# Top-k attention with a mixture of depths: the last keys turned into another bank, the scores in halves of 288 keys behind the values

## The chip, the cores and the metric

The kernel runs on one core of a Trainium2 chip. The core's engines work side by side, each through its own list of instructions in order, and wait for one another by semaphores: TensorE (matrix products and turns, results into PSUM), ScalarE (ACT), VectorE (DVE), GpSimd (POOL) and SyncE (SP, which issues transfers). The metric is device time in microseconds (us).

## The reference

Attention for 8 batches, 8 heads, 576 tokens of 64 numbers, all in float32. In each row of scores only the 32 largest count. Then a layer that works on the 128 tokens of a batch with the highest gate.

```
scores = q @ k.T / sqrt(64)
kth    = 32nd largest of each row
attn   = softmax(where(scores >= kth, scores, -1e9))
x      = concat over heads of attn @ v          # (8, 576, 512)
gate   = x @ w_gate
idx    = the 128 tokens of a batch with the largest gate
out    = x;  out[idx] = x[idx] + sigmoid(gate[idx]) * relu(x[idx] @ w1) @ w2
```

## The kernel before, in words

The work is cut into units `(b, t, hp)`: batch, query block and pair of heads, 8 x 5 x 4 = 160. For t = 0 to 3 a unit has two tiles, 128 queries of each head of the pair, by 576 keys. For t = 4 it has one, the last 64 queries of both heads together. J is 4, P is 128, R is 64, JP is 512, S is 576. Keys are taken as 512 ("0:JP") and the last 64 ("JP:S").

The main loop (line 590) is a pipeline written out by hand. In step `n` the engines do, for different units:

- TensorE, in this order: `turn` of z of unit n-3, tile 0 (four 128x128 transposes into `ptr`); `values` of unit n-4, tile 0 (products of pT and v into `av`); `turn` of tile 1; `turn_last`, which turns the last 64 keys of both tiles in one transpose; the scores of unit n+1 against 512 keys (`multiply`); `values` of tile 1; the scores against the last 64 keys. Then what a load step or a mixture step has.
- ScalarE: `part` (sides, the sign of score less bound) for n-1, the exponentials of n-3 (`pT` twice, then `last`), a first half of z for n-2, `keep` (scores of n+1 out of PSUM, `sc<-ps`), `keep_values` (`xs<-av`), then the copies of loads and mixture.
- GpSimd: `mask` for n-1 (y, with eight more numbers, "steps"), the second half of z for n-2, every fourth step `normalise` (x), then `cut` (`seen<-best`) for n and `lift` (`seen<-next`) for n-1.
- DVE: `find_bound` for n (32 largest by parts), `find_kth` for n-1, and parts of the mixture.

The next step's `sides` need this step's `cut`; z on ScalarE needs `lift`; z on GpSimd needs z on ScalarE; `turn` needs z on GpSimd.

PSUM has eight banks of 512 float32 a partition. The scores' tile `ps` has four (lines 84, 606), `ptr` two, `av` one, and one is shared in turn by the loads' turns and all steps of the mixture (`ps_misc`, tag "misc"). In `ps` the first tile's scores lie at 0 to 576, the second's at 1472 to 2048 (last 64 keys first), and `turn_last` writes at 896 to 1024, so into the bank that also has the first tile's last 64 keys:

```
tr = ps[0 : n * R, 1024 - P : 1024]
```

In nine of a batch's 20 steps the next batch's k and q are turned (`load_qkv`: TensorE `tr<-ident`, ScalarE `kqT<-tr`), and the mixture of the batch before goes on by one piece a step (`mixture`: xe_ps, extra_ps, h_ps twice, y_ps). Wrappers keep the program's order on TensorE, ScalarE, DVE and GpSimd (class `InOrder`); all their instructions stand under line 41 in the profile. The function `general` is a second way for inputs on which the fast search for the bound fails; it is not taken here.

Of the kernel before, what the change touches and what calls it, by code (L numbers as in the profile page):

```python
# [11 lines left out]
FP32 = mybir.dt.float32  # L12
# [32 lines left out]
def kernel(  # L45
# [104 lines left out]

    def room_for_qkv(b):

        return kqpool.tile([P, 2, NHP, S], FP32, name="kqT"), vbufs[b % 2]

    def load_qkv(qb, kb, vb, kqT, vs):

        last = [ldpool.tile([R, H, D], FP32, name=f"last{i}", bufs=1) for i in range(2)]
        for rows, src in zip(last, (kb, qb)):
            nc.sync.dma_start(out=rows, in_=src[:, JP:S, :].rearrange("h p d -> p h d"))

        def fetch(i):
            hp, src = i // 2, (kb, qb)[i % 2]
            rows = ldpool.tile([P, J, 2, D], FP32, name="rows")
            for hh in range(2):
                nc.sync.dma_start(
                    out=rows[:, :, hh, :],
                    in_=src[2 * hp + hh, 0:JP, :].rearrange("(p j) d -> p j d", j=J),
                )
            return rows

        fetched = [fetch(i) for i in range(3)]
        vt, vlast, vpair = vs
        v_rows = vb[:, JP:S, :].rearrange("h p d -> p h d")
        nc.sync.dma_start(out=vlast[:, :, 0:D], in_=v_rows)
        for hh in range(2):
            nc.sync.dma_start(
                out=vpair[hh * R : (hh + 1) * R, :, hh, 0:D], in_=v_rows[:, hh::2, :]
            )
        tr = ps_misc.tile([P, 512], FP32, name="tr", tag="misc")
        for i in range(2 * NHP):  # L180
            w, hp = divmod(i, NHP)
            pe.transpose(
                tr[:, i * R : (i + 1) * R],
                last[w][:, 2 * hp : 2 * hp + 2, :].rearrange("p h d -> p (h d)"),
                ident[0:R, 0:R],
            )
        act.copy(
            out=kqT[:, :, :, JP:S],
            in_=tr.rearrange("p (w c r) -> p w c r", w=2, c=NHP),
        )  # L190
        yield
        for i in range(2 * NHP):
            tr = ps_misc.tile([P, 512], FP32, name="tr", tag="misc")
            for c in range(J):
                pe.transpose(
                    tr[:, c * P : (c + 1) * P],
                    fetched[i][:, c, :, :].rearrange("p h d -> p (h d)"),
                    ident,
                )
            act.copy(out=kqT[:, i % 2, i // 2, 0:JP], in_=tr)  # L200
            if i + 3 < 2 * NHP:
                fetched.append(fetch(i + 3))
            nc.sync.dma_start(
                out=vt[:, i, :, 0:D],
                in_=vb[i, 0:JP, :].rearrange("(p j) d -> p j d", j=J),
            )
            yield

    def heads_of(t):

        return [[(0, 0), (1, R)]] if t == J else [[(0, 0)], [(1, 0)]]

    def multiply(t, hp, kqT, ps, keys):

        n = R if t == J else P
        for at, heads in zip((0, 1536) if keys.start == 0 else (JP, 1536 - R), heads_of(t)):
            for hh, r in heads:
                d = slice(hh * D, (hh + 1) * D)
                pe.matmul(
                    ps[r : r + n, at : at + keys.stop - keys.start],
                    kqT[d, 1, hp, t * P : t * P + n],
                    kqT[d, 0, hp, keys],
                )  # L230

    def keep(n, ps):

        sc = scpool.tile([P, 2, S], FP32, name="sc")
        for i in range(n):
            at = i * (4 * 512 - S)
            act.copy(out=sc[:, i, :], in_=ps[:, at : at + S])
        return sc

    def find_bound(n, sc):  # L240
# [69 lines left out]
            pe.transpose(tr[:, c * P : (c + 1) * P], z[:, i, at : at + P], ident)  # L310
        return tr

    def turn_last(n, z, ps):

        last = z.rearrange("p i s -> p (i s)")[:, JP : JP + n * R]
        tr = ps[0 : n * R, 1024 - P : 1024]
        pe.transpose(tr, last, ident)
        return tr

    def values(t, hp, i, pT, last, av, vs):  # L320

# [125 lines left out]
    def mixture(row0, x, gate, rank, exact=False):  # L447
# [51 lines left out]
        for t in range(NT):  # L499
            n = R if t == J else P  # L500
            pe.matmul(
                ps[:, 0:2],
                pick[0:n, t, :],
                extra[0:n, t, :],
                start=(t == 0),
                stop=(t == J),
            )
        row_i = modpool.tile([P, 1], I32, name="row_i", bufs=2)

        dve.tensor_scalar_min(out=row_i, in0=ps[:, 0:1], scalar1=float(B * S - 1))  # L510
        g = modpool.tile([P, 1], FP32, name="g")
        dve.tensor_copy(out=g, in_=ps[:, 1:2])

        hT = modpool.tile([P, NFC, CAP], FP32, name="hT")
        for f0 in range(0, NFC, 4):
# [19 lines left out]
                ps, hT[:, fc, :], w2[:, fc, :], start=(fc == 0), stop=(fc == NFC - 1)  # L535
            )
        gy = modpool.tile([P, HD], FP32, name="gy")
        act.activation(gy, ps, AF.Copy, scale=g)

        nc.gpsimd.indirect_dma_start(  # L540
            out=out.flatten_outer_dims(),
# [45 lines left out]
    def tiles_of(n):  # L587
        return len(heads_of(units[n][1])) if 0 <= n < len(units) else 0

    for n in range(-1, len(units) + 6):  # L590
# [11 lines left out]
        if tiles_of(n - 4):  # L602
            b4, t4, hp4 = units[n - 4]
            av = ps_av.tile([P, 512], FP32, name="av")
        if tiles_of(n - 3) or tiles_of(n + 1):
            ps = ps_sc.tile([P, 4 * 512], FP32, name="ps")
        for i in range(2):
            if i < tiles_of(n - 3):
                trs.append(turn(i, z))
                if i == tiles_of(n - 3) - 1:  # L610
                    trs.append(turn_last(i + 1, z, ps))
            if i == 1 and tiles_of(n + 1):
                b, t, hp = units[n + 1]
                multiply(t, hp, qkv[b][0], ps, slice(0, JP))
            if i < tiles_of(n - 4):
                values(t4, hp4, i, *weights[n - 4], av, qkv[b4][1])
        if tiles_of(n + 1):
            multiply(t, hp, qkv[b][0], ps, slice(JP, S))


        if tiles_of(n):
# [114 lines left out]
    def general_weights(n, sc):  # L736

        p = wkpool.tile([P, 2, S], FP32, name="p", tag="z")
        for i in range(n):
            cur, tops = sc[:, i, :], []  # L740
            left = wkpool.tile([P, 2, S], FP32, name="left", tag="z")
            for r in range(TOP_K // 8):
                tops.append(stats.tile([P, 8], FP32, name=f"top{r}"))
                nc.vector.max(tops[-1], cur)
                if r < TOP_K // 8 - 1:
                    nc.vector.match_replace(left[:, 0, :], tops[-1], cur, LOWEST)
                    cur = left[:, 0, :]
            shift = stats.tile([P, 1], FP32, name="shift")
            nc.vector.tensor_scalar_mul(shift, tops[0][:, 0:1], -scale)
            e = wkpool.tile([P, S], FP32, name="e", bufs=1)  # L750
            nc.scalar.activation(
                e, sc[:, i, :], AF.Exp, bias=shift, scale=scale
            )
            nc.vector.scalar_tensor_tensor(
                out=p[:, i, :],
                in0=sc[:, i, :],
                scalar=tops[-1][:, 7:8],
                in1=e,
                op0=ALU.is_ge,
                op1=ALU.mult,  # L760
            )
        return p

    def general(b, row0):
        def of(a):
            return a[bass.ds(b, 1)].rearrange("o a s d -> (o a) s d")

        kqT, vs = room_for_qkv(0)
        for _ in load_qkv(of(q), of(k), of(v), kqT, vs):
            pass  # L770
        x = xpool.tile([P, NT, HD], FP32, name="x")
        gate = xpool.tile([P, NT], FP32, name="gate")
        for t in range(NT):
            xs = xpool.tile([P, H, DE], FP32, name="xs")
            for hp in range(NHP):
                w = len(heads_of(t))
                ps = ps_sc.tile([P, 4 * 512], FP32, name="ps")
                for keys in (slice(0, JP), slice(JP, S)):
                    multiply(t, hp, kqT, ps, keys)
                p = general_weights(w, keep(w, ps))  # L780
                av = ps_av.tile([P, 512], FP32, name="av")
                pT = ptpool.tile([P, 2, J, P], FP32, name="pT")
                last = ptpool.tile([P, P], FP32, name="last")
                for i in range(w):
                    nc.scalar.copy(
                        out=pT[:, i, :, :],
                        in_=turn(i, p).rearrange("p (c i) -> p c i", c=J),
                    )
                nc.scalar.copy(out=last[0 : w * R, :], in_=turn_last(w, p, ps))
                for i in range(w):  # L790
                    values(t, hp, i, pT, last, av, vs)
                keep_values(t, hp, av, xs)
            rows = R if t == J else P
            den = stats.tile([P, H], FP32, name="den")
            normalise(rows, xs, x[0:rows, t, :], den)
            gates(t, x, gate)
# [44 lines left out]
```

## Time and profile before

| | us |
|---|---|
| median of 3 runs (1640.2 to 1644.38) | 1641.87 |
| the profiled execution | 1643.82 |
| its span, first to last instruction | 1641.9 |
| TensorE busy in it | 1293.2 (79%) |
| GpSimd busy | 969.5 (59%) |
| DVE busy | 884.5 (54%) |
| ScalarE busy | 861.0 (52%) |

Mean granted TensorE clock 0.739 of full speed; it has two levels, 0.5 (1.2 GHz) and 1.0 (2.4 GHz). A batch takes about 198 us. In the rows, PE is TensorE, "PE ptr<-ident,z" a turn of z, "PE ps<-kqT" scores, "ps<-ident,z" the turn of the last keys, "av" values; "[idle before <-releaser]" is how long the engine stood before and what ended it. Neighbouring instructions of a kind are one row with a count. One float32 product is two records, a turn one.

### The profile page before, as it was taken

How to read it: one execution, taken by the hardware profiler on the slowest of the kernel's cores; microseconds unless marked ns; L12 is line 12 of the kernel's file. 1: busy time of each engine (PE TensorE's matmuls, PEld its weight loads, DVE VectorE, ACT ScalarE, POOL GpSimd, SP SyncE). 2: the span in 40 equal slices, each digit the busy share in tenths (PEclk: the TensorE clock that was granted, in tenths of full speed). 3: DMA queues.
4: the chain of work that ended last, by engine and by line, in shares of the span. 5: the costliest groups of instructions: out<-in, count | busy, mean ns of one | idle time of the engine just before them, and what ended most of it. 6: DMA issues, size and time to landing. Idle time of an engine off the chain costs nothing.

```text
span 1641.9 us, 23197 instructions
## 1 busy us (share of the span) xinstructions
PE 1293.2 (79%) x6938; PEld 941.0 (57%) x6938; DVE 884.5 (54%) x4986; ACT 861.0 (52%) x1897; POOL 969.5 (59%) x1254
## 2 busy tenths in 40 slices
PE   4778867887678876798777987779877888779876
PEld 2555545665457654575555755566545665457564
DVE  5555356654665436663466534665357653665532
ACT  4555446554555545565455644655546554555530
POOL 4666557564666647665476654756557664666640
PEclk8566667796768867697576975779657795667868
DMA  8201120011100111001100112001120010000000
GB/s 208 49 7 27 26 58 4 13 33 27 55 1 18 35 42 34 1 20 34 55 20 1 27 33 55 14 4 24 39 58 4 4 36 1 26 4 1 7 27 12
DMA packets 123189, 46.92 MB, mean 29 GB/s; under 512 B 118832, under 2 KB 118832, under 8 KB 122032
## 3 DMA queue, kind: packets, MB, share of 16 engines
q1 hardware_dynamic: 121904, 43.27, 10.7%
q0 software_dynamic: 1152, 2.10, 1.0%
q8 instruction: 57, 0.93, 0.2%
q14 instruction: 76, 0.62, 0.1%
HBM read 33.82 MB, written 11.53 MB: 28 GB/s over the span
## 4 chain that ended last, share of the span: by engine, by line
PE 73%; POOL 14%; ACT 9%; issue 3%; DMA 1%; DVE 1%; ACTq 0%; SPq 0%; POOLq 0%
PE av L41 27%; PE ps L41 21%; PE ptr L41 14%; POOL z L41 12%; ACT z L41 6%; PE h_ps L41 4%; PE y_ps L41 3%; PE xe_ps L41 3%; POOL y L41 1%; PE tr L41 1%; POOL out_dram L540 1%; ACT sides L41 1%; ACT hT L41 1%; DMA rows<-in_q_dram 0%; ACT pT L41 0%
## 5 line engine op out<-in xcount | busy, mean ns | idle before, releaser
L41 POOL TENSOR_TENSOR z<-sc,z 128x576 f32<-128x576 f32 x288 | 405.6, 1426 | 375.2 <-ACT z L41 374.2
L41 PEld LDWEIGHTS av<-v,pT 128*128 128x128 f32 (+1 forms) x2560 | 403.6, 247 | 180.0 <-issue 170.1
L41 DVE MAX8 cand<-sc 128x8 f32<-128x72 f32 x2304 | 325.6, 218 | 334.9 <-ACT sc L41 334.5
L41 PE MATMUL ptr<-ident,z 128*128 128x128 f32 x1152 | 266.2, 374 | 293.5 <-POOL z L41 293.5
L41 POOL TENSOR_TENSOR y<-sc,sides 128x576 f32<-128x576 f32 x288 | 367.6, 1276 | 173.3 <-ACT sides L41 161.2
L41 PE MATMUL av<-v,pT 128*128 128x65 f32 (+1 forms) x2560 | 434.5, 332 | 0.4 <-ACT xs L41 0.4
L41 DVE MAX8 next<-y 128x8 f32<-128x584 f32 x288 | 220.5, 768 | 348.9 <-POOL y L41 348.9
L41 PEld LDWEIGHTS ptr<-ident,z 128*128 128x128 f32 x1152 | 188.8, 199 | 319.9 <-POOL z L41 318.4
L41 PE MATMUL ps<-kqT 64*128 64x64 f32 (+3 forms) x1280 | 350.2, 645 | 2.7 <-ACT kqT L41 2.7
L41 ACT ACTIVATE sides<-sc,seen 128x576 bf16<-128x576 f32 x288 | 221.0, 768 | 158.4 <-POOL seen L41 158.3
L41 ACT ACTIVATE last<-ps 128x128 f32<-128x128 f32 (+1 forms) x160 | 44.1, 276 | 437.8 <-PE ps L41 414.6
L41 ACT ACTIVATE z<-sc,seen 128x576 f32<-128x576 f32 x288 | 207.3, 764 | 0.2 <-POOL seen L41 0.2
L41 PEld LDWEIGHTS ps<-kqT 64*128 64x128 f32 (+1 forms) x1280 | 122.9, 230 | 89.4 <-issue 68.4
L41 ACT COPY sc<-ps 128x576 f32<-128x576 f32 x288 | 168.8, 633 | 5.0 <-PE ps L41 5.0
L41 ACT ACTIVATE pT<-ptr 128x512 f32<-128x512 f32 x288 | 159.7, 582 | 18.1 <-PE ptr L41 17.5
L41 DVE MAX8 best<-cand 128x8 f32<-128x64 f32 x864 | 154.6, 216 | 3.3
L41 DVE MATCH_REPLACE8 cand<-best,cand 128x64 f32<-128x64 f32 x576 | 116.5, 209 | 0.0
L41 POOL TENSOR_SCALAR y<-steps,seen 128x8 f32<-128x8 f32 x288 | 77.9, 271 | 22.6
L41 PE MATMUL tr<-ident,rows 128*128 128x128 f32 x256 | 46.4, 309 | 25.5 <-ACT hT L41 8.2
L41 PE MATMUL h_ps<-xeT,w 128*128 128x128 f32 x512 | 61.4, 278 | 1.1 <-ACT hT L41 0.7
L41 PE MATMUL av<-vpair,last 128*128 128x130 f32 x256 | 61.3, 324 | 0.0
L41 ACT COPY kqT<-tr 128x512 f32<-128x512 f32 x72 | 43.0, 598 | 33.6 <-PE tr L41 33.6
(72 smaller groups left out, 916.1 us busy)
## 6 DMA issues: line engine op xcount, KB each, us to landing
rows<-in_k_dram SPq DMA_DIRECT2D x64, 128.0 KB, 2.9
rows<-in_q_dram SPq DMA_DIRECT2D x64, 128.0 KB, 2.8
v<-in_v_dram SPq DMA_DIRECT2D x64, 128.0 KB, 2.8
out_dram<-x SPq DMA_DIRECT2D x8, 1024.0 KB, 4.3
w<-in_moe_w_dram SPq DMA_DIRECT2D x2, 2048.0 KB, 11.7
last<-in_k_dram SPq DMA_DIRECT2D x8, 128.0 KB, 3.0
last<-in_q_dram SPq DMA_DIRECT2D x8, 128.0 KB, 3.3
vlast<-in_v_dram SPq DMA_DIRECT2D x8, 128.0 KB, 3.1
```

The costliest lines, as they stand in the source:

```text
L41: return lambda *a, **kw: self._tc.keep_in_program_order(fn(*a, **kw))
L540: nc.gpsimd.indirect_dma_start(out=out.flatten_outer_dims(), out_offset=bass.IndirectOffsetOnAxis(ap=row_i, axis=0), in_=gy, in_offset=Non ...
```

## The change

The turn of the last keys goes into a tile of its own in the shared bank. `ps` is now two tiles by two halves of 512, of which 288 are used, each half in a bank of its own. So that both tiles can take 288 neighbouring keys in their order, k's last 64 tokens are stored twice, ahead of the 512 and behind them (kT), and q has its own tile. All four products of scores stand behind the values. In the mixture ScalarE copies the two picked columns out of the bank, which DVE did in two instructions. What is left out of the diff is the same change in `general`, and its calls.

```diff
     def room_for_qkv(b):
 
-        return kqpool.tile([P, 2, NHP, S], FP32, name="kqT"), vbufs[b % 2]
+        kT = kqpool.tile([P, NHP, R + S], FP32, name="kT")
+        qT = kqpool.tile([P, NHP, S], FP32, name="qT")
+        return kT, qT, vbufs[b % 2]
...
-        act.copy(
-            out=kqT[:, :, :, JP:S],
-            in_=tr.rearrange("p (w c r) -> p w c r", w=2, c=NHP),
-        )
+        tails = tr.rearrange("p (w c r) -> p w c r", w=2, c=NHP)
+        act.copy(out=kT[:, :, 0:R], in_=tails[:, 0, :, :])
+        act.copy(out=kT[:, :, S : S + R], in_=tails[:, 0, :, :])
+        act.copy(out=qT[:, :, JP:S], in_=tails[:, 1, :, :])
...
-            act.copy(out=kqT[:, i % 2, i // 2, 0:JP], in_=tr)
+            if i % 2 == 0:
+                act.copy(out=kT[:, i // 2, R:S], in_=tr)
+            else:
+                act.copy(out=qT[:, i // 2, 0:JP], in_=tr)
...
-    def multiply(t, hp, kqT, ps, keys):
+    def multiply(t, hp, kT, qT):
...
         n = R if t == J else P
-        for at, heads in zip((0, 1536) if keys.start == 0 else (JP, 1536 - R), heads_of(t)):
-            for hh, r in heads:
-                d = slice(hh * D, (hh + 1) * D)
-                pe.matmul(
-                    ps[r : r + n, at : at + keys.stop - keys.start],
-                    kqT[d, 1, hp, t * P : t * P + n],
-                    kqT[d, 0, hp, keys],
-                )
+        ps = ps_sc.tile([P, 2, 2, 512], FP32, name="ps")
+        for u in range(2):
+            for i, heads in enumerate(heads_of(t)):
+                at = u * HALF + (0 if i else R)
+                for hh, r in heads:
+                    d = slice(hh * D, (hh + 1) * D)
+                    pe.matmul(
+                        ps[r : r + n, i, u, 0:HALF],
+                        qT[d, hp, t * P : t * P + n],
+                        kT[d, hp, at : at + HALF],
+                    )
+        return ps
 
     def keep(n, ps):
 
         sc = scpool.tile([P, 2, S], FP32, name="sc")
         for i in range(n):
-            at = i * (4 * 512 - S)
-            act.copy(out=sc[:, i, :], in_=ps[:, at : at + S])
+            act.copy(
+                out=sc[:, i, :].rearrange("p (u s) -> p u s", u=2),
+                in_=ps[:, i, :, 0:HALF],
+            )
         return sc
...
-    def turn_last(n, z, ps):
+    def turn_last(n, z):
 
         last = z.rearrange("p i s -> p (i s)")[:, JP : JP + n * R]
-        tr = ps[0 : n * R, 1024 - P : 1024]
-        pe.transpose(tr, last, ident)
-        return tr
+        tr = ps_misc.tile([P, 512], FP32, name="last_ps", tag="misc")
+        pe.transpose(tr[0 : n * R, 0:P], last, ident)
+        return tr[0 : n * R, 0:P]
...
+        picked = modpool.tile([P, 2], FP32, name="picked")
+        act.copy(out=picked, in_=ps[:, 0:2])
         row_i = modpool.tile([P, 1], I32, name="row_i", bufs=2)
 
-        dve.tensor_scalar_min(out=row_i, in0=ps[:, 0:1], scalar1=float(B * S - 1))
-        g = modpool.tile([P, 1], FP32, name="g")
-        dve.tensor_copy(out=g, in_=ps[:, 1:2])
+        dve.tensor_scalar_min(out=row_i, in0=picked[:, 0:1], scalar1=float(B * S - 1))
...
-        act.activation(gy, ps, AF.Copy, scale=g)
+        act.activation(gy, ps, AF.Copy, scale=picked[:, 1:2])
...
-        if tiles_of(n - 3) or tiles_of(n + 1):
-            ps = ps_sc.tile([P, 4 * 512], FP32, name="ps")
         for i in range(2):
             if i < tiles_of(n - 3):
                 trs.append(turn(i, z))
                 if i == tiles_of(n - 3) - 1:
-                    trs.append(turn_last(i + 1, z, ps))
-            if i == 1 and tiles_of(n + 1):
-                b, t, hp = units[n + 1]
-                multiply(t, hp, qkv[b][0], ps, slice(0, JP))
+                    trs.append(turn_last(i + 1, z))
             if i < tiles_of(n - 4):
-                values(t4, hp4, i, *weights[n - 4], av, qkv[b4][1])
+                values(t4, hp4, i, *weights[n - 4], av, qkv[b4][2])
         if tiles_of(n + 1):
-            multiply(t, hp, qkv[b][0], ps, slice(JP, S))
+            b, t, hp = units[n + 1]
+            ps = multiply(t, hp, *qkv[b][0:2])
```

TensorE, one two-tile step without a load, before (ptr is the turn of z, ps<-ident,z the last keys' turn, ps<-kqT scores, av values):

```order
L41 MATMUL ptr<-ident,z 128x128 [waits Pool_49]
L41 MATMUL ptr<-ident,z 128x128 x3
L41 MATMUL av<-v_123,pT 128x65 [waits PE_49,Activation_49]
L41 MATMUL av<-v_123,pT 128x65 x3
L41 MATMUL ptr<-ident,z 128x128 [waits Pool_49]
L41 MATMUL ptr<-ident,z 128x128 x3
L41 MATMUL ps<-ident,z 128x128 [waits PE_49]
L41 MATMUL ps<-kqT 128x512 x2
L41 MATMUL av<-v_123,pT 128x65 x4
L41 MATMUL av<-vpair_127,last 128x130
L41 MATMUL ps<-kqT 128x64 x2
```

and now (last_ps is the last keys' turn):

```order
L41 MATMUL ptr<-ident,z 128x128 [waits Pool_49]
L41 MATMUL ptr<-ident,z 128x128 x3
L41 MATMUL av<-v_123,pT 128x65 [waits PE_49,Activation_49]
L41 MATMUL av<-v_123,pT 128x65 x3
L41 MATMUL ptr<-ident,z 128x128 [waits Pool_49]
L41 MATMUL ptr<-ident,z 128x128 x3
L41 MATMUL last_ps<-ident,z 128x128
L41 MATMUL av<-v_123,pT 128x65 x4
L41 MATMUL av<-vpair_127,last 128x130
L41 MATMUL ps<-kT,qT 128x288 [waits PE_49]
L41 MATMUL ps<-kT,qT 128x288 x3
```

The 512-key scores and the 64-key scores have become one group of four behind the values; the last keys' turn stays in its place but writes last_ps, and what the first write to ps waits for now stands at the scores.

ScalarE, one step with a load, before (sides, pT, last, z, then the scores' copy sc, the values' copy xs and the load's copy kqT):

```order
L41 ACTIVATE sides,seen<-sc,seen 128x576 [waits Activation_49,Pool_49]
L41 ACTIVATE sides,seen<-sc,seen 128x576 [waits Activation_49]
L41 ACTIVATE pT<-ptr 128x512 [waits PE_49] x2
L41 ACTIVATE last<-ps 128x128 [waits PE_49]
L41 ACTIVATE z<-sc,seen 128x576 [waits Pool_49]
L41 ACTIVATE z<-sc,seen 128x576
L41 COPY sc<-ps 128x576 [waits DVE_49,Activation_49]
L41 COPY xs<-av 128x130
L41 COPY kqT<-tr 128x512 [waits PE_49]
```

and now:

```order
L41 ACTIVATE sides,seen<-sc,seen 128x576 [waits Activation_49,Pool_49]
L41 ACTIVATE sides,seen<-sc,seen 128x576 [waits Activation_49]
L41 ACTIVATE pT<-ptr 128x512 [waits PE_49] x2
L41 ACTIVATE last<-last_ps 128x128 [waits PE_49]
L41 ACTIVATE z<-sc,seen 128x576 [waits Pool_49]
L41 ACTIVATE z<-sc,seen 128x576
L41 COPY sc<-ps 128x576 [waits DVE_49,PE_49,Activation_49]
L41 COPY xs<-av 128x130
L41 COPY kT<-tr 128x512 [waits PE_49]
```

The order is the same. `last` reads last_ps, and the scores' copy has a wait for TensorE of its own, which it did not have.

TensorE, a step with a load before it, before:

```order
L41 MATMUL ptr<-ident,z 128x128 [waits Pool_49]
L41 MATMUL ptr<-ident,z 128x128 x3
L41 MATMUL ps<-ident,z 128x128 [waits PE_49]
L41 MATMUL ps<-kqT 128x512 x2
L41 MATMUL av<-v_115,pT 128x65 x4
L41 MATMUL av<-vpair_119,last 128x130
L41 MATMUL ps<-kqT 128x64 x2
L41 MATMUL tr<-ident,rows 128x128 [waits DMAHW5_49,DMAHW4_49,Activation_49]
L41 MATMUL tr<-ident,rows 128x128 x3
```

and now:

```order
L41 MATMUL ptr<-ident,z 128x128 [waits Pool_49]
L41 MATMUL ptr<-ident,z 128x128 x3
L41 MATMUL last_ps<-ident,z 128x128 [waits Activation_49]
L41 MATMUL av<-v_115,pT 128x65 x4
L41 MATMUL av<-vpair_119,last 128x130
L41 MATMUL ps<-kT,qT 128x288 x4
L41 MATMUL tr<-ident,rows 128x128 [waits DMAHW5_49,DMAHW4_49,Activation_49]
L41 MATMUL tr<-ident,rows 128x128 x3
L41 MATMUL ptr<-ident,z 128x128 [waits PE_49,Pool_49]
```

The last keys' turn now waits for ScalarE, which empties the shared bank of the load's turn; the rest of the values and the scores stand behind it.

## Rows read from the trace of the kernel before

**Rows 1.** Table of waits: engine, line, awaited; us in total, times, longest.

```profile
ACT last L41 <- PE ps L41: 414.6, 148, 6.3
...
PE ptr L41 <- POOL z L41: 293.5, 132, 4.3
```

**Rows 2.** Timeline, TensorE: start, us, instruction, count [idle before, releaser].

```profile
664.85 1.12 PE L41 MATMUL ptr<-ident,z 128*128 128x128 f32 x4 [2.47 <-POOL z L41]
...
668.22 0.42 PE L41 MATMUL ps<-ident,z 128*128 128x128 f32 x1
668.56 2.08 PE L41 MATMUL ps<-kqT 64*128 64x512 f32 x4
...
671.96 0.44 PE L41 MATMUL ps<-kqT 64*128 64x64 f32 x4
```

**Rows 3.** Timeline, ScalarE, the same unit.

```profile
666.33 0.78 ACT L41 ACTIVATE sides<-sc,seen 128x576 bf16<-128x576 f32 x1 [1.00 <-POOL seen L41]
...
667.86 1.19 ACT L41 ACTIVATE pT<-ptr 128x512 f32<-128x512 f32 x2
672.45 0.28 ACT L41 ACTIVATE last<-ps 128x128 f32<-128x128 f32 x1 [3.39 <-PE ps L41]
672.62 1.43 ACT L41 ACTIVATE z<-sc,seen 128x576 f32<-128x576 f32 x2
673.95 1.17 ACT L41 COPY sc<-ps 128x576 f32<-128x576 f32 x2
```

**Rows 4.** Timeline, GpSimd, the same unit.

```profile
666.11 0.18 POOL L41 CAST seen<-best 128x2 f32<-128x2 bf16 x1
...
667.28 1.28 POOL L41 TENSOR_TENSOR y<-sc,sides 128x576 f32<-128x576 f32 x1 [0.67 <-ACT sides L41]
...
668.99 1.27 POOL L41 TENSOR_TENSOR y<-sc,sides 128x576 f32<-128x576 f32 x1
670.34 0.27 POOL L41 TENSOR_SCALAR y<-steps,seen 128x8 f32<-128x8 f32 x1
673.47 2.77 POOL L41 TENSOR_TENSOR z<-sc,z 128x576 f32<-128x576 f32 x2 [2.86 <-ACT z L41]
```

**Rows 5.** Stretches, TensorE: from:to, us, busy (count), clock, DMA, GB/s.

```profile
56.43:67.81 11.38, 8.86 (x36) 0.50 0.01 1
245.48:252.88 7.40, 4.88 (x35) 1.00 0.01 2
654.65:695.05 40.40, 30.37 (x141) 0.67 0.00 1
```

**Rows 6.** Timeline, GpSimd, end of the unit at clock 1.00.

```profile
251.43 2.78 POOL L41 TENSOR_TENSOR z<-sc,z 128x576 f32<-128x576 f32 x2 [0.18 <-ACT z L41]
```

**Rows 7.** Groups of instructions: GpSimd's x; busy us, mean ns, idle before.

```profile
L41 POOL TENSOR_TENSOR x<-xs,rden 128x512 f32<-128x512 f32 x32 | 33.4, 1045 | 0.3 <-DVE rden L41 0.3
```

**Rows 8.** Stretches, TensorE, first mixture unit of batch 1.

```profile
302.74:308.95 6.21, 6.21 (x24) 0.50 0.00 1
308.95:317.76 8.81, 8.14 (x62) 1.00 0.01 2
```

**Rows 9.** Stretches, TensorE, the parts of the sum.

```profile
38.19:199.96 161.77, 126.40 (x582) 0.65 0.14 29
893.24:949.70 56.46, 53.03 (x329) 0.91 0.09 20
949.70:988.41 38.71, 31.09 (x158) 0.69 0.18 37
988.41:1033.94 45.53, 32.92 (x167) 0.59 0.21 56
1033.94:1091.21 57.27, 42.28 (x215) 0.73 0.01 3
1487.16:1641.90 154.74, 122.57 (x700) 0.79 0.05 12
```

**Rows 10.** Timeline, DVE, beside GpSimd's first y.

```profile
667.87 0.21 DVE L41 MATCH_REPLACE8 cand<-best,cand 128x64 f32<-128x64 f32 x1
```

More of the change, by code (lines that the diff above doesn't have):

```diff
@@ L151, in room_for_qkv, with load_qkv @@
     def room_for_qkv(b):
-        return kqpool.tile([P, 2, NHP, S], FP32, name="kqT"), vbufs[b % 2]
-    def load_qkv(qb, kb, vb, kqT, vs):
+        kT = kqpool.tile([P, NHP, R + S], FP32, name="kT")
+        qT = kqpool.tile([P, NHP, S], FP32, name="qT")
+        return kT, qT, vbufs[b % 2]
+    def load_qkv(qb, kb, vb, kT, qT, vs):
         last = [ldpool.tile([R, H, D], FP32, name=f"last{i}", bufs=1) for i in range(2)]
@@ L749, in general_weights @@
             nc.vector.tensor_scalar_mul(shift, tops[0][:, 0:1], -scale)
-            e = wkpool.tile([P, S], FP32, name="e", bufs=1)
+            e = wkpool.tile([P, S], FP32, name="e", tag="sides")
             nc.scalar.activation(
@@ L766, in of @@
             return a[bass.ds(b, 1)].rearrange("o a s d -> (o a) s d")
-        kqT, vs = room_for_qkv(0)
-        for _ in load_qkv(of(q), of(k), of(v), kqT, vs):
+        kT, qT, vs = room_for_qkv(0)
+        for _ in load_qkv(of(q), of(k), of(v), kT, qT, vs):
             pass
@@ L776, in general @@
                 w = len(heads_of(t))
[L777 to L780, printed above, removed]
+                p = general_weights(w, keep(w, multiply(t, hp, kT, qT)))
                 av = ps_av.tile([P, 512], FP32, name="av")
@@ L788, in general @@
                     )
-                nc.scalar.copy(out=last[0 : w * R, :], in_=turn_last(w, p, ps))
+                nc.scalar.copy(out=last[0 : w * R, :], in_=turn_last(w, p))
                 for i in range(w):
```

## The prediction

> **What bounds the kernel now.** I read the table of waits first, then one unit of the steady loop engine by engine in the timeline, then busy time and granted clock by stretch. A unit is one step of the loop over `n`: two score tiles of 128 queries (one tile in the units with t = 4, the last 64 queries of two heads).
>
> The table of waits says ScalarE waits longest for the scores' bank: 414.6 us, 148 times, before `last`; and TensorE 293.5 us, 132 times, before it turns z [rows 1]. The timeline shows that these are one loop. TensorE turns the last keys at 668.22; that is done at 668.64. Then it goes on with scores and values and ends with the 64-key scores, 671.96 + 0.44 = 672.40 [rows 2]. ScalarE has had pT ready since 669.05, yet `last` starts at 672.45 after 3.39 us idle, released by "PE ps" [rows 3]. So `last` does not start behind the turn that it reads but behind everything TensorE does in the unit. Only then come ScalarE's z (672.62) and GpSimd's z (673.47, after 2.86 us idle) [rows 4], and TensorE starts the next unit some 2.5 us after its end (2.47 before the unit shown). A unit is thus TensorE's whole work plus a chain of 2.5 us in which TensorE stands.
>
> TensorE's work depends on its clock: 8.86 us in a unit at 0.50 (1.2 GHz), 4.88 us in one at 1.00 (2.4 GHz), for units of 11.38 and 7.40 us. Most units lie between: four in a row take 40.40 us at 0.67, 10.1 each with 7.59 of work [rows 5]. One row says what comes next: in the unit at 1.00 GpSimd is idle only 0.18 us before its z [rows 6]. At that clock GpSimd's loop already sets the pace, about 7.3 us.
>
> **The change part by part.**
>
> *Last keys into the other bank.* `last` now reads a tile of its own in the bank of loads and mixture. In the order, `keep` has gained a wait on TensorE that it did not need while `last`, in front of it, waited for the same thing; so `last` now waits for less. The row shows a wait of 3.8 us past the end of what is read (668.64 to 672.45). The Trainium skill, PSUM — Partial Sum Buffer, section Terms, says that TensorE and another engine may not be in one bank and quadrant at once; by that rule `last`, in the bank that also took the 64-key scores, had to stay clear of them, and in the new place it need not: the trace agrees (3.8 us), and by the rule the sum is the one below. Without it the sum is the same, and the chance that the wait stays is a little larger.
>
> With the wait gone ScalarE runs on: two `sides` 1.53 (666.33 to 667.86), pT 1.19, `last` 0.17 (672.45 to 672.62), the first z about 0.75, 3.6 us from the first `sides` to z's end [rows 3]. GpSimd is later than that: from `cut` (666.11) to its first y 1.17 us, from there to the end of the second y's steps 3.33 us (667.28 to 670.61) [rows 4], then z 2.77 us, then the next `cut`: 1.17 + 3.33 + 2.77 = 7.27 us. That is the loop that ends last in a two-tile unit. Once per four units x is normalised between z and `cut`, 1.05 us [rows 7], 0.26 a unit. Sum 7.53.
>
> *TensorE beside it.* It starts a unit when the first z is there, 1.6 us before the first `sides` (half of GpSimd's 2.77 and 0.22 from `cut` to `sides`). At 2.4 GHz 4.9 us of work are done 3.3 us after it, ahead of `keep`, which ScalarE reaches 4.3 us after it (3.6 and the rest of 1.43 for both z): hidden. At 1.2 GHz 8.86 us end 7.3 us after `sides`; `keep` (1.17) and a short copy of av follow, so the next `sides` comes at about 8.6 instead of 7.3, and the next values wait for that av (one buffer). The dense work before raised the clock: TensorE busy from 302.74 at 0.50 got 1.00 at 308.95 [rows 8]. Removing 2.5 us of standing per unit makes such stretches more frequent, and at 2.4 GHz it catches up. A unit half at each clock needs 2 / (1/8.86 + 1/4.88) = 6.3 us, under 7.3. I add 0.17 us a unit for late `keep`s and for ScalarE's load copies in the units that have them: 7.7 us.
>
> *Halves of 288.* The keys are 576 as before; a unit has eight matmul records 288 wide in place of four of 512 and four of 64. These took 2.08 and 0.44 us [rows 2]; on the line between the two widths four of 288 take 1.26, so 2.52 before and 2.52 after: nothing. No row shows that width. Bounds: the closing 64-wide group no longer stands by itself (0.44 us less), or it costs in every pass what four narrow records cost beyond their columns (0.44 us more). Both lie beside GpSimd's loop at 2.4 GHz. I take 0.
>
> *Scores follow values.* The end of TensorE's unit stays where it was, so `keep` is not later; the values no longer wait behind the 512-key scores. Nothing at 2.4 GHz.
>
> *Extra copies.* k's tails: three copies per batch instead of one; `picked` on ScalarE instead of a DVE copy; once per batch each, well under 1 us together beside 198 us. ScalarE is not the bound; 0, at most 8 us in all.
>
> *New wait.* TensorE's turn of the last keys needs the bank of loads free: in nine units a batch ScalarE copies k or q from it, and the mixture has its steps there. Behind the waiting turn stand the rest of the values and the scores. ScalarE's copy comes after `keep` and av, which end 1.4 us after the scores, and takes about as long as a score copy, half of 1.17: 2.0 us. TensorE has turns and values of 3.4 us (664.85 to 668.22, at 1.2 GHz) or half of that before it wants the bank. So 0 to 0.3 us, in the 0.17.
>
> *Sum by stretch* [rows 9]. 38.19 to 199.96, 16 two-tile units: 161.8 to 16 x 7.7 = 123.2, saves 39. Then per batch: (a) five steps around the one-tile units, 45.5 us: GpSimd's loop is 5.6 with one y less (1.71), 5.9 with one z less (1.38), 4.2 with both, so 5.6 + 3 x 4.2 + 5.9 and some x, 25; TensorE's 32.9 busy us at 0.59 would be about 27 at three quarters of the clock; I take 28.5, saves 17. (b) six two-tile units, 57.3 to 46.2, saves 11. (c) mixture, 56.5 us with 53.0 busy on TensorE at 0.91: TensorE bounds it, saves 1.5. (d) four two-tile units, 38.7 to 30.8, saves 8. (a) and (b) occur seven times, (c) and (d) six times before 1487.16: 7 x 28 + 6 x 9.5 = 253. The end, 154.7 us: four two-tile units (9), the last one-tile units (6), the mixtures nothing: 15. In all 39 + 253 + 15 = 307. The profiled execution took 1643.8 us (span 1641.9); 1643.8 - 307 = 1337, and the median shown, 1641.9, lies 0.1% below that execution: 1336.
>
> **The rivals.**
> A: TensorE becomes the bound at its present mix of clocks. A unit then is 7.59 us of work plus 0.7 for the wait on av: 8.3. By stretch as above that saves 29 + 7 x (14 + 7.5) + 6 x 7 + 10 = 232, time 1412. At 1.2 GHz throughout the two-tile units (8.86 + 0.7 = 9.6) little but the one-tile saving is left, about 1530. For it: 8.86 is over 7.3. Against: rows 8.
> B: no lag at all, 7.4 a unit, and the mixture at 1.00 instead of 0.91 (a unit at 0.91 takes 1 / (0.18/8.86 + 0.82/4.88) = 5.3 us, so its 53.0 become 53.0 x 4.88 / 5.3 = 49): 307 + 0.3 x 86 + 7 x 4 = 361, so 1283.
> C: GpSimd slows beside DVE, since the two now work closer together. If the four replacements of 0.21 us that DVE makes in a unit held GpSimd up for their whole time, 0.84 us a unit in 86 units are 72 us, time 1408. Against: y takes 1.28 us beside such replacements and 1.27 beside none [rows 4, 10]. The Trainium skill, GPSIMD Engine Reference, section Key points, says that the two engines share their SBUF ports, with contention when a DVE instruction has two inputs there or runs in a two-port mode; here the trace shows none of it (1.28 against 1.27).
> D: the wait stays, because `last` now waits for something else written to the bank. Against: the order has no other writer between turn and `last`. Then about 1642.
> E, slower: the work is spread so that the clock no longer rises in the mixture. The place is stretch (c): its 53.0 busy us at 0.91 would be 53.0 x 8.86 / 5.3 = 89 at 0.50, 35 more in each of seven batches, 248, against 114 still saved elsewhere: about 1780. It decides when the mixture's mean clock falls below about 0.7. Against: TensorE is busy 94% of that stretch, in long rows without a wait.
>
> **How the numbers follow.** Forecast with B's side of it 0.74 (1283 to 1380), A and C 0.17, D 0.04, E 0.05. Range 1280 to 1420: it takes A's first case and C, and leaves the all-1.2-GHz case, D and E outside. A measurement of this kernel tells a change from none at about 0.3%, 5 us. Faster 0.91, same 0.04, slower 0.05.
>
> **What would show it.** Right: ScalarE's wait for "PE ps" before `last` gone from the table, or turned into a short one on its own turn; GpSimd's z directly behind its y; two-tile units of 7.3 to 7.9 us; the mixture stretch near 55 us; GpSimd with the largest share in the chain of waits there. Wrong: TensorE without idle time in units over 8 us at 0.5 (A); y or z on GpSimd longer than 1.28 and 1.43 (C); `last` still starting after the scores (D); a lower clock in the mixture (E).

## The result and the profile after

The changed kernel takes 1372.3 us (median of 4 runs, 1366.4 to 1379.8), the kernel before 1643.1 (4 runs, 1640.2 to 1646.2): ratio 0.8354, 95% interval 0.8307 to 0.8401. The forecast was 1336, its range 1280 to 1420. The profiled execution took 1366.4 us, its span is 1364.4, and the mean granted clock 0.823. The four runs differ by 1%, and their time follows their clock: 1366.4 at 0.823, 1369.9 at 0.817, 1374.7 at 0.812, 1379.8 at 0.800. So the profile shows the fastest of the four, 6 us under the median.

The table of waits of the changed kernel comes first (columns as in [rows 1]):

```profile
POOL y L41 <- ACT sides L41: 216.3, 160, 11.8
PE ptr L41 <- POOL z L41: 177.7, 103, 4.6
ACT sides L41 <- POOL seen L41: 152.0, 96, 3.4
ACT sc L41 <- issue: 91.7, 47, 2.5
...
POOL z L41 <- ACT z L41: 10.2, 22, 1.4
```

The largest row of before, `last` behind "PE ps" with 414.6 us [rows 1], is gone. GpSimd's wait for ScalarE's z is 10.2 us now; before it was

```profile
POOL z L41 <- ACT z L41: 374.2, 149, 6.4
```

A new row appears, 91.7 us of ScalarE standing before `sc`, the scores' copy ("issue" means that the view names no releaser). The next two fences are GpSimd and ScalarE in two units, the first with TensorE at 2.4 GHz and the second with TensorE at 1.2 (start, duration):

```profile
70.78 0.19 POOL L41 CAST seen<-best 128x2 f32<-128x2 bf16 x1
...
71.96 1.28 POOL L41 TENSOR_TENSOR y<-sc,sides 128x576 f32<-128x576 f32 x1 [0.67 <-ACT sides L41]
...
75.02 0.27 POOL L41 TENSOR_SCALAR y<-steps,seen 128x8 f32<-128x8 f32 x1
75.38 2.77 POOL L41 TENSOR_TENSOR z<-sc,z 128x576 f32<-128x576 f32 x2
78.10 0.18 POOL L41 CAST seen<-best 128x2 f32<-128x2 bf16 x1
...
85.41 1.04 POOL L41 TENSOR_TENSOR x<-xs,rden 128x512 f32<-128x512 f32 x1
```

```profile
80.94 0.27 ACT L41 ACTIVATE last<-last_ps 128x128 f32<-128x128 f32 x1
81.09 1.44 ACT L41 ACTIVATE z<-sc,seen 128x576 f32<-128x576 f32 x2
85.07 1.18 ACT L41 COPY sc<-ps 128x576 f32<-128x576 f32 x2 [2.54 <-issue]
86.14 0.29 ACT L41 COPY xs<-av 128x130 f32<-128x130 f32 x1
```

They answer to [rows 3, 4]. `last` starts directly behind pT, with no idle time (3.39 us before). GpSimd's z starts directly behind y's steps (2.86 us idle before), and from one `seen` to the next are 78.10 - 70.78 = 7.32 us, where 7.27 was worked out. TensorE in the same units:

```profile
72.70 1.24 PE L41 MATMUL ps<-kT,qT 64*128 64x288 f32 x8
76.83 1.11 PE L41 MATMUL ptr<-ident,z 128*128 128x128 f32 x4 [2.89 <-POOL z L41]
...
82.69 2.29 PE L41 MATMUL ps<-kT,qT 64*128 64x288 f32 x8
84.91 1.11 PE L41 MATMUL ptr<-ident,z 128*128 128x128 f32 x4
...
86.47 1.11 PE L41 MATMUL av<-v,pT 128*128 128x65 f32 x8 [0.45 <-ACT xs L41]
```

In the first unit TensorE is done early and waits 2.89 us for z: GpSimd ends last. In the second it turns without a pause at 84.91, after 8.08 us (76.83 to 84.91); there it ends last itself. ScalarE stands 2.54 us before `sc`, which starts at 85.07, just behind the end of the scores at 84.98; the copy xs comes behind it, and the next values wait 0.45 us for xs.

The stretches answer to [rows 9] (from:to, us, TensorE busy and count, clock):

```profile
39.59:158.90 119.31, 96.53 (x582) 0.78 0.18 37
...
158.90:189.68 30.78, 22.15 (x168) 0.89 0.34 87
189.68:236.39 46.71, 30.58 (x216) 0.93 0.02 4
236.39:289.67 53.28, 49.38 (x330) 0.94 0.09 21
...
397.29:456.41 59.12, 55.55 (x329) 0.83 0.08 19
728.16:744.56 16.40, 15.72 (x83) 0.69 0.00 0
751.42:763.91 12.49, 11.80 (x74) 0.73 0.10 22
```

The first 16 two-tile units take 119.3 us (161.8 before), the five one-tile steps of batch 1 30.8 (45.5), its six two-tile units 46.7 (57.3). The mixture of the second batch, 59.1 us, is longer than before's 56.5, and its clock lower, 0.83 against 0.91.

From the starts of TensorE's turns I sorted all steps into three kinds. One-tile steps are those with the turn or the values of a one-tile unit; steps with mixture pieces stand apart:

| sum in us, mean clock | 86 two-tile steps | 38 one-tile steps | 35 mixture steps |
|---|---|---|---|
| before | 831, 0.70 | 333, 0.59 | 391, 0.91 |
| after | 651, 0.79 | 231, 0.83 | 391, 0.87 |

The whole gain is in the steps without mixture: 180 and 102 us. The mixture gave nothing. In the experiments below these three sums are each from the one profiled execution of the kernel in question.

### The profile page after: what moved, and what is told of

It is laid out like the page before. It is cut to its first block, busy times and chain, and to the rows that moved or that the text cites. A ratio compares the mean times of both kernels' runs of the same rounds, so it can differ in the third digit from the quotient of the medians.

```text
span 1364.4 us, 23293 instructions
## 1 busy us (share of the span) xinstructions
PE 1111.4 (81%) x6938; PEld 885.7 (65%) x6938; DVE 910.9 (67%) x4978; ACT 853.6 (63%) x1921; POOL 983.1 (72%) x1254
## 5 line engine op out<-in xcount | busy, mean ns | idle before, releaser
L41 POOL TENSOR_TENSOR y<-sc,sides 128x576 f32<-128x576 f32 x288 | 368.8, 1281 | 226.6 <-ACT sides L41 216.3
L41 POOL TENSOR_TENSOR z<-sc,z 128x576 f32<-128x576 f32 x288 | 413.3, 1454 | 21.3 <-ACT z L41 10.2
L41 PE MATMUL av<-v,pT 128*128 128x65 f32 (+1 forms) x2560 | 379.8, 304 | 13.2 <-ACT xs L41 13.2
L41 PEld LDWEIGHTS av<-v,pT 128*128 128x128 f32 (+1 forms) x2560 | 362.1, 223 | 32.2 <-ACT xs L41 25.0
L41 PE MATMUL ptr<-ident,z 128*128 128x128 f32 x1152 | 227.7, 331 | 178.2 <-POOL z L41 177.7
L41 PEld LDWEIGHTS ptr<-ident,z 128*128 128x128 f32 x1152 | 160.8, 174 | 233.9 <-POOL z L41 228.0
L41 PE MATMUL ps<-kT,qT 64*128 64x288 f32 (+1 forms) x1280 | 252.2, 524 | 2.7 <-ACT qT L41 2.7
L41 ACT COPY sc<-ps 128x576 f32<-128x576 f32 x288 | 171.7, 646 | 122.1 <-issue 91.7
L41 PEld LDWEIGHTS ps<-kT,qT 64*128 64x128 f32 (+1 forms) x1280 | 128.2, 218 | 57.8 <-issue 13.7
L41 PE MATMUL av<-vpair,last 128*128 128x130 f32 x256 | 68.8, 357 | 0.0
L41 PEld LDWEIGHTS tr<-ident,rows 128*128 128x128 f32 x256 | 31.0, 158 | 58.1 <-issue 16.1
L41 PEld LDWEIGHTS h_ps<-xeT,w 128*128 128x128 f32 x512 | 60.8, 198 | 8.7 <-issue 3.6
```

The source lines that it names most:

```text
L41: return lambda *a, **kw: self._tc.keep_in_program_order(fn(*a, **kw))
```

## Experiments

**Only the bank.** The kernel before, with one edit:

```diff
-        tr = ps[0 : n * R, 1024 - P : 1024]
-        pe.transpose(tr, last, ident)
-        return tr
+        tr = ps_misc.tile([P, 512], FP32, name="last_ps", tag="misc")
+        pe.transpose(tr[0 : n * R, 0:P], last, ident)
+        return tr[0 : n * R, 0:P]
```

> The kernel before with one edit: the last keys are turned into the bank of loads and mixture; scores stay 512 + 64 keys, around the second values. Theory (the bank move alone ends the wait of `last`): 1355 to 1390 us, ScalarE's 415 us before `last` gone, two-tile units of 7.3 us where TensorE has 2.4 GHz. Rival (halves and order carry a good part): above 1420 us.

1379.1 us (1376.8 to 1380.2), ratio 0.8387 [0.8372, 0.8402]. ScalarE has no row for `last` behind "PE ps" any more, GpSimd's wait for z is small, and where TensorE has 2.4 GHz there are two-tile units of 7.3 us, beside shorter and longer ones (5.6 to 8.3):

```profile
ACT sc L41 <- issue: 119.3, 56, 3.6
POOL z L41 <- ACT z L41: 11.6, 29, 1.5
```

The bank's edit alone gives as much as the whole change; the two intervals overlap. The last experiment shows that this does not make the other parts worth nothing.

**All but the bank.** The changed kernel, with the last keys turned into the scores' bank of the first tile again:

```diff
-        tr = ps_misc.tile([P, 512], FP32, name="last_ps", tag="misc")
+        tr = ps[0 : n * R, 0, 1, 384:512]
...
+            ps = ps_sc.tile([P, 2, 2, 512], FP32, name="ps")
```

> The changed kernel with the last keys turned into an unused corner of the scores' tile, in a bank that takes scores in the same step; halves of 288, the doubled tail of k, the order and `picked` stay. Theory: `last` waits for the last scores again, 1610 to 1660 us, ScalarE's wait for TensorE before `last` 390 us or more. Rival (halves and order help by themselves): below 1560 us.

1659.0 us (1653.9 to 1663.9), ratio 1.0088 [1.0059, 1.0116]. The waits are back:

```profile
ACT last L41 <- PE ps L41: 440.5, 149, 5.7
POOL z L41 <- ACT z L41: 384.2, 146, 5.8
```

Halves, order and copies with the wait left in place don't help: the kernel is 0.9% slower, at a mean clock of 0.682 to 0.692 (0.734 to 0.745 before). Why the clock is lower was not tested. One unit, TensorE and then ScalarE, shows what `last` waits for:

```profile
461.61 2.29 PE L41 MATMUL ps<-kT,qT 64*128 64x288 f32 x8
463.95 0.28 ACT L41 ACTIVATE last<-ps 128x128 f32<-128x128 f32 x1 [3.37 <-PE ps L41]
```

`last` starts 0.05 us behind the end of the last product, 463.90. That product is the second tile's (`ps[.., 1, 1]`), in another bank than the one that `last` reads (`ps[.., 0, 1]`); the products into its own bank end at 463.42.

**Scores first again.** The changed kernel with its four products of scores ahead of the second tile's values:

```diff
+            if i == 1 and tiles_of(n + 1):
+                b, t, hp = units[n + 1]
+                ps = multiply(t, hp, *qkv[b][0:2])
             if i < tiles_of(n - 4):
                 values(t4, hp4, i, *weights[n - 4], av, qkv[b4][2])
-        if tiles_of(n + 1):
-            b, t, hp = units[n + 1]
-            ps = multiply(t, hp, *qkv[b][0:2])
```

> The changed kernel with one edit: all four score products stand between the last keys' turn and the second values, so `keep` need not wait for the end of TensorE's unit. Theory of late `keep`s (units at 1.2 GHz take 8.1 to 8.6 instead of 7.3 us because `keep` and the copy of av come behind the scores): those units get 0.3 to 0.8 us shorter, 1350 to 1368 us. Rival (TensorE's own 8.1 us bound these units, the order is worth nothing): 1368 to 1382 us.

1330.8 us (1324.1 to 1333.9), ratio 0.8093 [0.8071, 0.8115]: more than either theory said. ScalarE's wait before `sc` fell, but that was not the main gain:

```profile
ACT sc L41 <- issue: 23.7, 14, 2.4
```

```profile
257.15:266.40 9.25, 8.56 (x74) 1.00 0.14 31
413.95:423.20 9.25, 8.56 (x73) 1.00 0.13 30
```

The first fence is from the table of waits (91.7 in the changed kernel), the second two stretches, the first of the two mixture steps with h_ps in two batches. The two-tile steps went from 651 to 645 us only; the mixture went from 391 to 364, its first h step at full clock in five of seven batches (12.49 us at 0.73 in the stretch of the changed kernel above). So 27 of the 39 us between the two profiled executions lie in the mixture, whose mean clock is 0.95 instead of 0.87, and 6 in the two-tile steps.

**`cut` ahead of z.** On GpSimd `cut` for unit n stands before z of n-2, so that the next `sides` overlap z:

```diff
+        if tiles_of(n):
+            cut(tiles_of(n), bests.pop(n), first_tile[n])
         if tiles_of(n - 2):
             sc = scs.pop(n - 2)
...
-        if tiles_of(n):
-            cut(tiles_of(n), bests.pop(n), first_tile[n])
         if tiles_of(n - 1):
```

> The changed kernel with one edit: on GpSimd `cut` stands before z instead of behind it (and behind x), so the next `sides` need not wait for z. Theory (GpSimd's loop of 7.31 us through z and `cut` bounds two-tile units at 2.4 GHz): those units fall to about 6.7 us, GpSimd's waits for `sides` (216 us) mostly go, 1310 to 1350 us. Rival (TensorE's work and clock bound the kernel as a whole, mean clock goes up only a little): 1355 us or more.

1318.4 us (1316.6 to 1321.5), ratio 0.8026 [0.8011, 0.8040]. The timeline of GpSimd, and TensorE's stretch of the same unit:

```profile
186.47 0.22 POOL L41 TENSOR_SCALAR seen<-next 128x2 f32<-128x2 f32 x1
186.76 1.28 POOL L41 TENSOR_TENSOR y<-sc,sides 128x576 f32<-128x576 f32 x1
...
190.16 0.18 POOL L41 CAST seen<-best 128x2 f32<-128x2 bf16 x1
190.31 2.78 POOL L41 TENSOR_TENSOR z<-sc,z 128x576 f32<-128x576 f32 x2
```

```profile
185.06:191.77 6.71, 4.43 (x35) 1.00 0.01 2
```

GpSimd no longer waits 0.67 us for `sides`; the unit is 6.71 us instead of 7.32, at full clock and with 2.3 us in which TensorE stands. So GpSimd's loop bounds such units. The two-tile steps went from 651 to 611 us, the mixture from 391 to 383. That GpSimd's waits for `sides` mostly go did not come true: 163.5 of 216.3 us are left, in 82 waits instead of 160.

**Both of these.**

> The changed kernel with both edits: scores between the last keys' turn and the second values, and `cut` before z on GpSimd. Theory (the two bounds are separate: GpSimd's loop at 2.4 GHz, and the clock of the mixture with late `keep`s): the savings of 41 and 54 us add up, 1265 to 1295 us. Rival (both take away the same waiting): 1300 to 1320 us.

1289.4 us (1286.4 to 1291.5), ratio 0.7846 [0.7834, 0.7857]. The two gains nearly add: 1372.3 - 41.4 - 53.9 would be 1277. But they do not lie in the two places that the expectation named. Beside an early `cut` the order takes 20 us off the two-tile steps (611 to 591) and 6 off the one-tile steps (229 to 223), and only 1 off the mixture (383 to 381), where by itself it took 27. What the order is worth, and where, depends on the rest of the kernel.

**y's steps on DVE.** The two edits above, and the eight extra numbers of y moved off GpSimd:

```diff
         pool.tensor_tensor(y[:, i, 0:S], sc[:, i, :], sides[:, i, :], ALU.mult)
-        pool.tensor_scalar(
+        dve.tensor_scalar(
             out=y[:, i, S : S + 8],
```

> As the kernel with both edits, and the eight step numbers of y (128x8, 0.27 us and 0.09 us to the next, twice in a two-tile unit) are made by DVE instead of GpSimd. Theory (GpSimd's list is still the bound where TensorE has 2.4 GHz): two-tile units there go from 6.7 to about 6.0 us, 20 to 45 us less than with both edits. Rival (TensorE's 8.1 us at 1.2 GHz and ScalarE's 5.9 are the bound now): within 10 us of it.

1226.8 us (1225.8 to 1233.2), ratio 0.7478 [0.7461, 0.7494], the fastest of all kernels here, ahead of before and of the changed kernel (0.7478 / 0.8354 = 0.895; from the ends of the two intervals, 0.888 to 0.902). Busy time and shares of the span, then GpSimd, then a two-tile unit:

```profile
PE 1023.0 (84%) x6938; PEld 800.1 (65%) x6938; DVE 1016.4 (83%) x5266; ACT 853.3 (70%) x1921; POOL 895.8 (73%) x966
```

```profile
168.86 2.53 POOL L41 TENSOR_TENSOR y<-sc,sides 128x576 f32<-128x576 f32 x2
171.32 0.20 POOL L41 CAST seen<-best 128x2 f32<-128x2 bf16 x1
171.47 2.78 POOL L41 TENSOR_TENSOR z<-sc,z 128x576 f32<-128x576 f32 x2
```

```profile
167.16:172.94 5.78, 4.62 (x36) 1.00 0.02 6
```

Both y now stand back to back. The saving against the version without this edit, 62.6 us, is over the 20 to 45 expected: two-tile steps 591 to 552, one-tile 223 to 214, and the mixture 381 to 369, which GpSimd doesn't bound.

**The picked columns on DVE.** Only that part of the change undone, since the mixture had not gained:

```diff
-        picked = modpool.tile([P, 2], FP32, name="picked")
-        act.copy(out=picked, in_=ps[:, 0:2])
...
+        g = modpool.tile([P, 1], FP32, name="g")
+        dve.tensor_copy(out=g, in_=ps[:, 1:2])
```

> The changed kernel with one edit: in the mixture DVE reads the two picked columns out of the bank, as before the change, and ScalarE's copy is gone. Theory (the 0.74 us that TensorE stands for that copy is what lets the clock fall behind the extra unit, so that the first h unit takes 12.5 to 14 us instead of 11.4): that unit 9.2 to 11.4 us, 1348 to 1364 us in all. Rival (the clock falls there by where in its swing the unit comes, not by that wait): 1366 to 1382 us.

1369.6 us (1363.4 to 1376.0), ratio 0.8337 [0.8312, 0.8361], as the changed kernel. The first h step still takes 12.5 to 13.7 us in four of the six full batches. The copy is not the cause.

**Scores twice.** In the seven steps ahead of each mixture TensorE does its scores two times into the same tile, the same numbers again:

```diff
+            quiet = n >= NHP and 3 <= n % per_batch < 10
+            ps = multiply(t, hp, *qkv[b][0:2], times=2 if quiet else 1)
```

> The changed kernel with more work: in seven steps per batch ahead of the mixture's matmuls TensorE makes the four score products twice (same results, 1.2 us more at 2.4 GHz, 2.2 us at 1.2). Theory (TensorE standing 2.9 us in a unit at 2.4 GHz is what drops its clock, and that costs the next units and the mixture): those steps stay at 2.4 GHz and 7.3 us, the xe unit 13.7 instead of 15 to 16.4 us, 1340 to 1364 us in spite of the added work. Rival (TensorE's work is what costs): 1374 us or more.

1352.6 us (1351.3 to 1355.1), ratio 0.8232 [0.8221, 0.8244]: more work, and 19.7 us less time. The two-tile steps are unchanged (651), the mixture fell from 391 to 369. That the seven steps stay at 2.4 GHz came true only in part: their mean clock rose from 0.75 to 0.82. Its first step with xe_ps ran at full clock in six of seven batches, as here; 16.40 us at 0.69 in the stretch of the changed kernel above:

```profile
403.10:416.80 13.70, 11.33 (x83) 1.00 0.01 2
```

So the mixture lost in the changed kernel through the clock, and the clock depends on what TensorE does before it.

**512 and 64 keys, together behind the values.** The bank's edit alone, with both products of scores in one place; no halves, no tails stored twice, no picked copy:

```diff
-            if i == 1 and tiles_of(n + 1):
-                multiply(t, hp, qkv[b][0], ps, slice(0, JP))
...
+            multiply(t, hp, qkv[b][0], ps, slice(0, JP))
             multiply(t, hp, qkv[b][0], ps, slice(JP, S))
```

> The kernel with the bank move alone (512 and 64 keys), and one edit more: the 512-key scores stand directly ahead of the 64-key scores, behind the values; no halves, no doubled tail. Only the halves then separate it from the changed kernel, whose unit takes TensorE 4.42 us at 2.4 GHz and 8.15 at 1.2, against 4.88 and 8.85 before. Theory (one group instead of two saves the gain, halves are worth nothing): 4.4 to 4.6 and 8.1 to 8.4 us a unit, 1360 to 1380 us in all. Rival (the halves save it): 4.75 us and more, 8.7 and more, 1376 us or more.

1352.0 us (1347.8 to 1356.9), ratio 0.8227 [0.8207, 0.8248]. TensorE's scores at either clock, and the first step with h_ps of one batch:

```profile
74.90 1.30 PE L41 MATMUL ps<-kqT 64*128 64x512 f32 x8
...
84.87 2.40 PE L41 MATMUL ps<-kqT 64*128 64x512 f32 x8
```

```profile
425.66:435.00 9.34, 8.65 (x74) 1.00 0.13 30
```

One group of 512 and 64 takes 1.30 and 2.40 us, eight records of 288 take 1.24 and 2.29: the halves are worth 0.06 to 0.11 us a unit, and standing in one group is worth the rest of what TensorE's unit lost (4.88 [rows 5] to 4.48). The time is outside both expectations: the mixture takes 369 us, its first h step at full clock in six of seven batches.

This run parts the sum of the whole change. With 512 and 64 keys, scores behind the values are 27 us better than scores around them (1352.0 against 1379.1). Halves, doubled tails and the picked copy on top of that cost 20 us (1372.3, interval 0.8307 to 0.8401 against 0.8207 to 0.8248). Without the picked copy 18 us are left (1369.6), and they are in the mixture, 388 against 369 us. No run parts the halves from the doubled tails.

## Why the prediction was right, and where it fell short

**The wait of `last`, and what is late next: right.** The row is gone, GpSimd's loop is 7.32 us (7.27 worked out), x adds its 1.04, and the bank alone gives a ratio of 0.8387 where the whole change gives 0.8354. Rival D is refuted. The theory that GpSimd bounds the units at 2.4 GHz stands by the experiment that shortened its loop: 6.71 us with 2.3 us of TensorE idle. The sign named for the chain of waits can't be judged, since the page follows that chain over only 27% of the span (TensorE 16%, GpSimd 6%).

The reason given for the wait says more than the rows show. The prediction named the scores' bank as the reason and took the 3.8 us as agreeing. But `last` starts behind the last product of the group (672.40 and 672.45 in [rows 2, 3]), which is the second tile's at 1472 to 1536, a bank that `last` does not read; the run without the bank's edit shows the same. Among the scores' records, the only update of the semaphore that `last` waits for stands at this last product. So the length of the wait was set by the last product into the tile. Whether a tile of its own in the scores' own bank would have been enough, no run shows; the edit changes tile and bank together.

**TensorE at 1.2 GHz, the next `sides` late: right in kind.** 8.08 us to the next turn, with ScalarE standing 2.54 us before `sc` and the values 0.45. The lag was put at 0.17 us a unit beyond 7.53, 7.70 in all. The mean of all two-tile steps is 651 / 86 = 7.57, but that has the short units of (d) in it; the first 16 units and (b) together take 454.3 / 58 = 7.83, so there the lag was too small by 0.13. Rival A is refuted as a whole, since TensorE stood 178 us for z, but in some units it is what happens, as (b) shows.

**The sum by stretch.** Predicted 307, measured 1641.9 - 1364.4 = 277.5 on the spans:

| part | predicted saving | measured |
|---|---|---|
| first 16 units, with 1.4 us later start | 39 | 42.5 - 1.4 = 41.1 |
| (a) one-tile steps, 7 times | 119 | 318.7 - 217.6 = 101.1 |
| (d) four units, 6 times | 48 | 228.9 - 166.2 = 62.7 |
| (b) six units, 7 times | 77 | 400.9 - 335.0 = 65.9 |
| (c) mixture, 6 times | 9 | 338.8 - 342.1 = -3.3 |
| the end from 1487.16 (before) | 15 | 154.7 - 144.6 = 10.1 |

(a) and (d) together were right, 167 against 163.8; only their border was drawn wrong. The stretches are cut at TensorE's units, but GpSimd works on units one and two steps ahead, so that TensorE's last units of (d) already go with GpSimd's short loop. (b) was mis-sized by 11: its mean unit is 7.98 instead of 7.70. Batches 1 and 5 come near the 46.2 predicted, with 46.7 each; the other five take 48.0 to 49.0, because their first two units run at 1.2 GHz with TensorE busy nearly throughout and take 8.1 to 8.2 and 9.4 to 9.7 us. This is the second of them in batch 2:

```profile
357.34:366.72 9.38, 8.93 (x42) 0.53 0.06 14
```

So it is the lag at 1.2 GHz that was too small. x costs its share too: in batch 1 two of the six units have one, not one and a half, and the last took 8.69 us (227.70 to 236.39), 1.04 of it for x and 0.34 for x's wait for DVE (7.31 without).

**(c), the mixture: the term that failed.** I took 1.5 us saved per batch from TensorE "busy 94% of that stretch"; the stretches of six batches came out between 53.3 and 59.1 us, on average 0.5 longer. TensorE still bounds them, but its clock is lower in them. In these six batches the step with xe_ps took 15.02 us at 0.79 before, and now 13.7 to 16.4, with less than 0.79 in four; the first with h_ps took 11.37 at 0.85 before and now 10.9 at 0.84 once and 12.5 to 14.1 at 0.64 to 0.73 in five. This is rival E's mechanism at a small size (0.87 instead of 0.91, far from its 0.7), while the forecast had put none of it into (c). That the clock is the cause is shown from one side: more work in the steps ahead brought the mixture to 369 us. Why it stays up in the first h step with 512 and 64 keys behind the values (9.34 us) or with halves ahead of them (9.25), and falls with halves behind them, is not settled; the picked copy is not it.

**Halves at nothing: wrong.** A unit is 4.42 us instead of 4.88 at 2.4 GHz, and about 8.1 instead of 8.86 at 1.2: 0.46 and 0.7 us, at the lower bound given (-0.44) or past it. The measured reason is one group in place of two, not the width. At 2.4 GHz the gain is covered by GpSimd's loop, as said. In the time, halves and doubled tails together cost 18 us (1369.6 against 1352.0), through the mixture.

**Order at nothing: wrong.** "The end of TensorE's unit stays where it was" held, yet scores ahead of the values are 41 us better. With 512 and 64 keys, behind the values is 27 us better than around them. Two terms were thus put at nothing that are worth some 27 us less and 20 us more, and they nearly cancel. That the time of the whole change lies so near that of the bank's edit alone is luck.

**Rival C, GpSimd beside DVE: small, but there.** y takes 1281 ns on average (1276 before), z 1454 (1426): 288 x (0.005 + 0.028) = 9.5 us of the 72 that C would have cost. It isn't in the replacements that the prediction looked at. It is in one DVE instruction with two inputs, `prod`, once in four units. Before, then now, GpSimd's row first and DVE's second:

```profile
454.98 3.24 POOL L41 TENSOR_TENSOR z<-sc,z 128x576 f32<-128x576 f32 x2 [0.78 <-ACT z L41]
454.92 0.67 DVE L41 CUSTOM_DVE_ANT_0 prod<-x,wg 64x512 f32<-64x512 f32 x1
```

```profile
806.03 3.22 POOL L41 TENSOR_TENSOR z<-sc,z 128x576 f32<-128x576 f32 x2 [0.46 <-ACT z L41]
806.29 1.70 DVE L41 CUSTOM_DVE_ANT_0 prod<-x,wg 128x512 f32<-128x512 f32 x1
```

Two z beside it take 3.2 us instead of 2.77. Where `prod` starts first, as at 454.92, it keeps its 0.67 us and the z takes some 1.85 instead of 1.41. Where a z starts first, as at 806.03, that z keeps its 1.41 us, `prod` ends 0.54 us behind it, and the next z, begun beside `prod`, takes 1.85. Before, 14 of 288 z were lengthened so and `prod` took 690 ns on average; now it is 31 z and 1294 ns. The Trainium skill, GPSIMD Engine Reference, section Key points, names DVE instructions with two inputs in SBUF as contending with GpSimd. The prediction said that the trace of before shows none of it; at y and the replacements that is so, at `prod` both traces show it.

## What to carry to other kernels

Look at what an engine waits for, and when that was written: a read that starts 3.8 us after the write of its own data waits for a neighbour in the same tile, and another buffer for 128 columns was worth 16% here. When such a wait goes, the next loop can be added up from single rows of the old trace (7.27 against 7.32), but cut the sum where the engine that will be the bound stands, not where the old one does. A stretch that is bound by TensorE should not be priced at its old clock when the work ahead of it changes: here that was 12 of the 30 us that the forecast missed. And a total that comes out near the forecast does not show that the parts put at nothing are nothing: here they were worth 27 us one way and 20 the other.

## What was not expected of the hardware

- TensorE's clock made a kernel with more work faster: scores done twice in seven steps a batch, 1352.6 us instead of 1372.3, mean clock 0.860 to 0.866 instead of 0.800 to 0.823.
- Eight 64-row score records of 512 and 64 keys in one group take 1.30 us at 2.4 GHz; as two groups of four, apart, they took 1.13 and 0.44 in the kernel with the bank's edit alone.
- Of DVE's `prod` and GpSimd's z, each with two inputs, the one that starts first keeps its time and the other is lengthened: `prod` from 0.67 to 1.3 us in most cases and 1.70 at most, a z from 1.41 to 1.85.
